# An attention and mixture-of-experts kernel: experts in the order of their token counts, with 448, 416 or 384 slots by place, and addresses from a register

## The chip, the cores and the metric

The kernel runs on one core of one Trainium2 chip. The metric is device time in microseconds of one execution. A run of three executions and one profiled execution are shown; an execution's time is some microseconds more than its span in the profile, which goes from the first to the last instruction.

The engines are named as in the profile: PE (TensorE, matmuls; PEld is its weight load), DVE (VectorE), ACT (ScalarE), POOL (GpSimd) and SP (SyncE, which here only issues DMAs and reads registers). L75 is line 75 of the kernel before.

## The reference

A gated linear attention gives x, and a mixture of eight experts with one expert per token follows. Cut to what matters:

```python
# attention: q, k, v, a_re, a_im are (4, 8, 768, 48)
for t in range(S):                       # state S_re, S_im: (B, H, D, D)
    S_re, S_im = ar * S_re - ai * S_im + outer(k[t], v[t]), ar * S_im + ai * S_re
    y[:, :, t] = einsum('bhd,bhde->bhe', q[:, :, t], S_re)
x = y.transpose(0, 2, 1, 3).reshape(3072, 384)
# experts: w_gate (384, 8), w1 (8, 384, 1024), w2 (8, 1024, 384)
logits = x @ w_gate
expert_idx = argmax(logits, axis=1)
gate_w = softmax(logits)[arange(N), expert_idx]
for e in range(8):
    rows = expert_idx == e
    out[rows] = gate_w[rows] * (relu(x[rows] @ w1[e]) @ w2[e])
```

`setup_inputs()` sets the seed 0, so the inputs are always the same. All data are float32.

## The kernel before

**Attention.** The 3072 tokens are 24 tiles of 128, taken in pairs ("units", 12 of them). Each unit's decays and angles are summed with matmuls against triangular matrices, q and k are scaled and rotated, and chunk scores, outputs and the running state are made by matmuls. A tile's output is transposed into rows of x (tile `x`) and multiplied by the gate weights (`logits`, L341), whose four matmuls write four strips of 32 partitions.

**Routing.** Four tiles form a group, six groups in all. `choose` (L352) finds each token's expert (`fst`) and its gate weight (`gt`); `route` (L373) counts tokens per expert with one-hot rows, running sums in `cx` and two matmuls into `rps`, and gives each token a row of the DRAM table `xs`: expert times 448 plus its rank. `put` (L407) scatters the rows of a tile to `xs` with an indirect DMA on POOL, four puts a group. The last group is routed when the experts have begun: the first 256 rows of the first expert (`FIRST`) are gathered before it, and `base` makes sure that late tokens get ranks from 256 on.

**Experts.** Every expert has `CAP` = 448 slots, as three tiles of 128 and one of 64, and the experts run in the order 0 to 7. For each of them `gather` (L488) reads its rows from `xs` into `xg`, `turn` (L589) transposes them on PE (tile `tp`) and copies them to `xt`, and `expert` (L615) runs two layers. The first makes eight tiles `hps` of 128 hidden units by 448 tokens, three matmuls each, with relu into `ht` on ACT and DVE in turn. The second makes one tile `yps` per 128 tokens, eight matmuls of 384 columns each. In the tile of 64 tokens the eight matmuls are split over two halves of the output partitions, four in each, which a copy on ACT and an add on DVE bring together (L646, L647). DVE multiplies by the gate weight, and `scatter` (L605) writes the rows to the output with an indirect DMA on POOL. The first expert is run in two parts, of 256 and 192 slots.

**Weights.** An expert's weights are 1.5 MB for `w1t` and 1.5 MB for `w2t`, in two sets of buffers. Those of expert 0 come in seven DMAs, one per unit from the fifth to the eleventh unit (L566); those of expert 1 before the experts start; the others two experts ahead, each buffer as soon as its last reader has ended (L712). All of these, the inputs and the gathers go through SP's queue, in one order that a scheduler sets from the order of the program.

**Checks on the side.** `range_check` (L666) tests the inputs' range on ACT and POOL while experts 1 to 6 run. `verdict` (L685) joins its result and the tokens that found no slot (`ov`) into `flag`, with one small matmul (`bp`). After the last expert every engine reads `flag`; if it isn't zero, spare code runs (`slow_attention`, `others`), which takes each expert over all 24 tiles. 

## Time and profile before

| | |
|---|---|
| Runs before | 620.66 us median of 3 (620.58 to 621.86) |
| Profiled execution | 620.54 us, span 618.8 us, 8535 instructions, granted PE clock 0.988 |
| PE busy | 563.5 us (91%), 3319 records; PEld 369.7 (60%) |
| DVE, ACT, POOL busy | 264.6 (43%), 284.5 (46%), 104.0 (17%) |
| DMA | 79.73 MB, mean 129 GB/s |
| `hps` matmuls | 148.4 us busy, 432 records |
| `yps` matmuls | 147.2 us busy, 512 records |

A float32 matmul leaves two records in the trace, so 432 records of `hps` are 216 matmuls. The busy time of a group counts overlapping records once, while the mean of one record has the time in which it overlaps with the next; so the cost of a matmul is read from the starts of consecutive blocks, not from that mean. A timeline row gives start, length, engine, line, operation, tile, shapes and the number of records merged; what stands in brackets is idle time ahead and what ended it. In a row of stretches the numbers in parentheses count instructions, and behind POOL stand the granted PE clock (1.00 is 2.4 GHz, 0.50 is 1.2 GHz), the mean busy share of the 16 DMA engines and GB/s.

### The profile page before, as it was taken

To read this page: it belongs to the slowest core of one execution; us is meant where nothing else is said; L and a number is where in the kernel's file an instruction comes from. 1 tells how busy PE (TensorE), PEld (TensorE's weight loads), DVE (VectorE), ACT (ScalarE), POOL (GpSimd) and SP (SyncE) were. 2 spreads that over 40 slices of the span, in tenths; PEclk is the share of its full clock that TensorE was granted. 3 is DMA by queue.
4 is the path that set the end of the run, shared out by engine and by line. 5 is a ranking of instruction groups with operands and counts; after the bars stand their busy time and mean duration, and the time that the engine had idled before them with its cause. 6 is when DMAs were issued, how large, how long until landed. Compare 5 with 4: busy or idle time off the path is not lost. (4 is left out here: it accounts for less than half of the span.)

```text
span 618.8 us, 8535 instructions
## 1 busy us (share of the span) xinstructions
PE 563.5 (91%) x3319; PEld 369.7 (60%) x3319; DVE 264.6 (43%) x579; ACT 284.5 (46%) x479; POOL 104.0 (17%) x100
## 2 busy tenths in 40 slices
PE   1498799899899899998899999999999999999993
PEld 0176588677677677776766554555555555455551
DVE  2567787787787779781312112121121211211111
ACT  6558876865865866743101161341613416134100
POOL 1000000100200200302120042140521405214011
PEclk9999999999999999999799999999999999999997
DMA  9996965575476251161125636426364263610000
GB/s 183 208 263 129 269 144 99 137 149 109 111 142 118 77 117 27 43 215 53 51 73 176 229 114 236 140 62 228 114 236 138 64 225 114 239 40 33 2 13 32
DMA packets 154232, 79.73 MB, mean 129 GB/s; under 512 B 130230, under 2 KB 145735, under 8 KB 154184
## 3 DMA queue, kind: packets, MB, share of 16 engines
q1 hardware_dynamic: 147008, 69.48, 43.7%
q0 software_dynamic: 3456, 9.47, 4.4%
q10 hardware_dynamic: 3720, 0.16, 0.3%
q8 instruction: 28, 0.46, 0.3%
q14 instruction: 20, 0.16, 0.1%
HBM read 63.74 MB, written 15.98 MB: 129 GB/s over the span
## 5 line engine op out<-in xcount | busy, mean ns | idle before, releaser
L75 PE MATMUL hps<-xt,w1t 128*128 128x448 f32 (+2 forms) x432 | 148.4, 504 | 0.0
L75 PE MATMUL yps<-w2t,ht 128*128 128x384 f32 (+1 forms) x512 | 147.2, 488 | 0.3 <-DVE y L639 0.3
L75 PEld LDWEIGHTS yps<-w2t,ht 128*128 128x128 f32 (+1 forms) x512 | 81.4, 177 | 64.4 <-issue 15.0
L75 PEld LDWEIGHTS hps<-xt,w1t 128*128 128x128 f32 x432 | 80.7, 192 | 61.9 <-issue 59.0
L624 ACT ACTIVATE ht<-hps 128x448 f32<-128x448 f32 (+2 forms) x36 | 18.1, 502 | 137.0 <-PE hps L75 137.0
L408 POOL DMA_INDIRECT xs<-x,to x24 | 26.6, 1107 | 284.4 <-DMA fl<-f 109.4
L639 DVE TENSOR_SCALAR y<-yps,xg 128x384 f32<-128x384 f32 x24 | 14.8, 617 | 118.4 <-PE yps L75 118.4
L628 DVE TENSOR_SCALAR ht<-hps 128x448 f32<-128x448 f32 (+2 forms) x36 | 20.6, 573 | 104.3 <-PE hps L75 103.0
L75 PE MATMUL at<-qt,kt 96*128 96x128 f32 x384 | 53.5, 282 | 0.8 <-ACT kt L78 0.7
L75 PEld LDWEIGHTS at<-qt,kt 96*128 96x128 f32 x384 | 47.9, 192 | 10.2 <-DVE kt L78 3.1
L75 PE MATMUL y<-am,v 128*64 128x128 f32 x384 | 50.6, 285 | 3.5 <-DVE am L438 3.4
L606 POOL DMA_INDIRECT out_dram<-y,xg x32 | 30.9, 966 | 94.1 <-DVE y L639 45.3
L438 DVE TENSOR_TENSOR am<-at,tri 128x512 f32<-128x512 f32 x48 | 33.0, 688 | 26.2 <-PE at L75 26.2
L75 PE MATMUL y<-qt,G 96*64 96x128 f32 x320 | 42.9, 278 | 0.0
L75 PE MATMUL csl<-A,tri_half 128*128 128x384 f32 x48 | 24.2, 590 | 20.5 <-DVE A L248 17.9
L677 POOL TENSOR_TENSOR cs<-cs,cw 128x768 f32<-128x768 f32 x12 | 21.6, 1804 | 117.4 <-ACT cw L673 117.4
L430 PE MATMUL tp<-ident,Q 128*96 128x128 f32 x192 | 33.7, 285 | 8.1 <-DVE Q L338 6.8
L75 PEld LDWEIGHTS y<-am,v 128*64 128x64 f32 x384 | 31.6, 135 | 14.4 <-issue 7.7
L78 ACT COPY qt<-tp 96x512 f32<-96x512 f32 x48 | 27.5, 583 | 21.5 <-PE tp L430 21.3
L201 ACT ACT_TABLE_LOAD x27 | 34.6, 1283 | 2.0 <-PEq L858 0.8
L430 PE MATMUL tp<-ident,K 128*96 128x128 f32 x192 | 30.8, 279 | 1.5 <-DVE K L338 1.5
L75 PE MATMUL dk<-v,K 128*96 128x48 f32 x320 | 32.2, 253 | 0.0
(122 smaller groups left out, 715.3 us busy)
## 6 DMA issues: line engine op xcount, KB each, us to landing
w1t<-in_moe_w_dram SPq DMA_DIRECT2D x7, 1536.0 KB
w2t<-in_moe_w_dram SPq DMA_DIRECT2D x7, 1536.0 KB
xs<-zrow SPq DMA_DIRECT2D x7, 772.0 KB
ar<-in_a_re_dram SPq DMA_DIRECT2D x12, 384.0 KB
ai<-in_a_im_dram SPq DMA_DIRECT2D x12, 384.0 KB
q<-in_q_dram SPq DMA_DIRECT2D x12, 384.0 KB
k<-in_k_dram SPq DMA_DIRECT2D x12, 384.0 KB
v<-in_v_dram SPq DMA_DIRECT2D x12, 384.0 KB
```

The costliest lines, as they stand in the source:

```text
L75: return nc.tensor.matmul(o, lhsT=lhsT, rhs=rhs, start=start, stop=stop, skip_group_check=True)
L78: (nc.scalar.copy if i % 2 else nc.vector.tensor_copy)(out=o, in_=in_)
L201: ins = nc.scalar.preload_act_table_set(name)
L408: pool(nc.gpsimd.indirect_dma_start(out=xs[:, :], out_offset=bass.IndirectOffsetOnAxis(ap=to[:, i : i + 1], axis=0), in_=x[:, i], in_offse ...
L430: nc.tensor.transpose(out=tp[0:DD, j], in_=X[:, hg * 4 + j], identity=ident)
L438: nc.vector.tensor_tensor(out=am, in0=at, in1=bc(tri, 1, 4), op=OP.mult)
L606: return nc.gpsimd.indirect_dma_start(out=out, out_offset=bass.IndirectOffsetOnAxis(ap=idx, axis=0), in_=y[0:m], in_offset=None, bounds_ch ...
L624: relu = nc.scalar.activation(out=ht[:, f], in_=ps, func=AF.Relu)
L628: nc.vector.tensor_scalar(out=ht[:, f], in0=ps, scalar1=0.0, scalar2=None, op0=OP.max)
L639: nc.vector.tensor_scalar(out=y, in0=ps, scalar1=gate, scalar2=None, op0=OP.mult)
L677: nc.gpsimd.tensor_tensor(out=s, in0=s, in1=w, op=OP.add)
```

## The change

The experts no longer run in the order of their numbers. A ranking by token counts sets the order, and the place in it sets the slots: `CAPS` = 448 for the first two, 416 for the next three, 384 for the last three. The table `xs` keeps 448 rows per expert.

- `rank` makes the order on DVE, on one partition, in some ten small steps: it compares all counts with each other, sums to a place per expert, and turns places into a list of experts. It runs twice. The first time, in the routing of the fourth group, it takes the counts of the first 16 tiles and fixes the first two experts (`order` 0); `bonus` keeps them ahead in the second ranking, which takes all counts (`used`) after the last group and fixes the other six (`order` 1). One small matmul into a further column of `rps` gives the counts each time.
- `experts_at` reads the numbers of the experts into registers of SP, two before the first weights, six after the first expert has been written into the program. `load_w` and `gather` address weights and rows by these registers.
- The first expert's weights are no longer spread over seven units: they are all loaded in the last unit, behind the two register loads.
- A place with 416 slots has a last tile of 32 tokens. `expert` splits its eight matmuls over four strips of 32 partitions, two in each, and joins them by a copy and three adds. A place with 384 slots has three full tiles and no other.
- `verdict` also flags an expert that has more tokens than its place has slots. `route` keeps the token's row in `slot` for the spare code, which is adapted and not shown here.

```diff
+    CAPS = [CAP] * 2 + [CAP - 32] * 3 + [CAP - 64] * 3
+    BIG = 32768.0
...
+    ex = []
+
+    def rank(cnt, some):
+
+        tt = nc.vector.tensor_tensor
+        key = xl.tile([1, E], FP, tag="key", name="key")
+        nc.vector.scalar_tensor_tensor(out=key, in0=cnt, scalar=8.0, in1=rev[0:1], op0=OP.mult, op1=OP.add)
+        if not some:
+            tt(out=key, in0=key, in1=bonus, op=OP.add)
+        w = xl.tile([1, E, E], FP, tag="kw", name="kw")
+        tt(out=w, in0=bc(key, 1, E), in1=bc(key, 2, E), op=OP.is_gt)
+        nc.vector.reduce_sum(place_of, w, axis=AX_X)
+        if some:
+            nc.vector.tensor_scalar(
+                out=bonus, in0=place_of, scalar1=-BIG, scalar2=2.0 * BIG, op0=OP.mult, op1=OP.add
+            )
+            nc.vector.tensor_scalar(out=bonus, in0=bonus, scalar1=0.0, scalar2=None, op0=OP.max)
+        w = xl.tile([1, E, E], FP, tag="kw", name="kw")
+        tt(out=w, in0=bc(place_of, 1, E), in1=bc(eid[0:1], 2, E), op=OP.is_equal)
+        tt(out=w, in0=w, in1=bc(eid[0:1], 1, E), op=OP.mult)
+        key = xl.tile([1, E], FP, tag="key", name="key")
+        nc.vector.reduce_sum(key, w, axis=AX_X)
+        nc.vector.tensor_copy(out=order[not some], in_=key)
+
+    def experts_at(i, some):
+
+        for e in i:
+            ex.append(nc.values_load(order[not some][0:1, e : e + 1], engines=[mybir.EngineType.SP], min_val=0, max_val=E - 1))
+
     def load_w(e, parts=None):
...
-        w1e, w2e = w1[e].rearrange("(i p) f -> p i f", p=P), w2[e].rearrange("(i p) d -> p i d", p=P)
+        w1e, w2e = [w[ds(ex[e], 1)].rearrange("o (i p) f -> p (o i) f", p=P) for w in (w1, w2)]
...
             mm(ps[:, n], ones_b, cx[:, j])
...
+            mm(ps[0:1, n + 1], ones_b[:, 0:1], cx[:, NT])
...
-        to = xl.tile([P, n], I32, tag="to", name="to")
+        to = slot[:, sl]
         stt(out=to, in0=far, scalar=float(NS), in1=rk, op0=OP.add, op1=OP.add)
+        if j == NT - 3 * GR:
+            mm(ps[0:1, n + 1], ones_b[:, 0:1], cx[:, j + n])
+            rank(ps[0:1, n + 1], True)
...
+        def last():
+            tt(out=used, in0=ps[0:1, n + 1], in1=base[0:1], op=OP.subtract)
+            rank(used, False)
...
-        return [lambda i=i: put(i) for i in range(n)]
+        return [lambda i=i: put(i) for i in range(n)] + ([last] if end else [])
...
-    def gather(s, sizes):
+    def gather(e, s, sizes):
...
-        nc.sync.dma_start(out=xg[:, :f], in_=xs[s : s + f * P].rearrange("(i p) c -> p i c", p=P))
+        rows = xs[0:NS].rearrange("(e s) c -> e s c", s=CAP)[ds(ex[e], 1), s : s + sum(sizes)]
+        nc.sync.dma_start(out=xg[:, :f], in_=rows[:, : f * P].rearrange("o (i p) c -> p (o i) c", p=P))
         if f < n:
-            nc.sync.dma_start(out=xg[0 : sizes[f], f], in_=xs[s + f * P : s + f * P + sizes[f]])
+            nc.sync.dma_start(out=xg[0 : sizes[f], f], in_=rows[:, f * P :].rearrange("o p c -> (o p) c"))
...
-        if NU - 8 <= u < NU - 1:
-            load_w(0, [u - (NU - 8)])
+        if u == NU - 1:
+            experts_at(range(2), True)
+            load_w(0, range(KD + KF // 2))
...
-                for f in range(KF // 2):
-                    for z in range(2):
-                        g = z * (KF // 2) + f
-                        mm(ps[z * HT : (z + 1) * HT], h[:, g], wb[:, g], f == 0, f == KF // 2 - 1)
-                nc.scalar.copy(out=y[0:m], in_=ps[HT : HT + m])
-                nc.vector.tensor_tensor(out=y[0:m], in0=ps[0:m], in1=y[0:m], op=OP.add)
+                zs = P // m
+                for f in range(KF // zs):
+                    for z in range(zs):
+                        g = z * (KF // zs) + f
+                        mm(ps[z * m : (z + 1) * m], h[:, g], wb[:, g], f == 0, f == KF // zs - 1)
+                nc.scalar.copy(out=y[0:m], in_=ps[m : 2 * m])
+                for z in [0] + list(range(2, zs)):
+                    nc.vector.tensor_tensor(out=y[0:m], in0=ps[z * m : (z + 1) * m], in1=y[0:m], op=OP.add)
...
+        for i in (2, 5):
+            w = xl.tile([1, E], FP, tag="key", name="key")
+            ts(out=w, in0=place_of, scalar1=float(i), scalar2=32.0, op0=OP.is_ge, op1=OP.mult)
+            nc.vector.tensor_tensor(out=used, in0=used, in1=w, op=OP.add)
+        ts(out=used, in0=used, scalar1=float(CAP), scalar2=None, op0=OP.is_gt)
...
+        nc.vector.reduce_sum(over, used, axis=AX_X)
+        nc.vector.tensor_tensor(out=two[0:1, 1:2], in0=two[0:1, 1:2], in1=over, op=OP.add)
...
-            part = [(own, xg)]
+            part = [(tiles(CAPS[e]), xg)]
...
-                xg = gather((e + 1) * CAP, own)
+                xg = gather(e + 1, 0, tiles(CAPS[e + 1]))
...
             expert(sizes, xt, *W_T[e], g, todo)
+        if e == 0:
+            experts_at(range(2, E), False)
         if e + 2 < E:
             load_w(e + 2)
```

**How it moves instructions on SP.** These are SP's rows where the attention ends, from the last load of v on. `w1t` and `w2t` with all parts in one DMA (128x3x1024, 128x8x384) are the second expert's weights, `xg` with 128x2x386 is the first gather, `own0`, and the two `xg` rows behind it are the gather of the first expert's second part. Before:

```order
L215 DMA v_96<-in_v_dram 128x16x48
L166 DMA w1t<-in_moe_w_dram 128x3x1024
L167 DMA w2t<-in_moe_w_dram 128x8x384
L493 DMA xg<-xs 128x2x386
L493 DMA xg<-xs 128x386
L495 DMA xg<-xs 64x386
```

Now (of the seven DMAs of the first expert's weights the first, and of the six register loads the first):

```order
L253 DMA v_96<-in_v_dram 128x16x48
L193 TENSOR_LOAD order_122
L193 ISA x2
...
L209 ISA
L209 DMA w1t<-in_moe_w_dram 128x1024
...
L540 DMA xg<-xs 128x2x386
L204 ISA
L204 DMA w1t<-in_moe_w_dram 128x3x1024
L205 ISA
L205 DMA w2t<-in_moe_w_dram 128x8x384
L193 TENSOR_LOAD order_123
...
L540 DMA xg<-xs 128x386
```

The first expert's weights have come down from the attention to this place, behind the register loads; the second expert's weights, which stood ahead of `own0`, stand behind it; and six register loads stand ahead of the gather of the second part.

**On DVE, the fourth group's routing.** `rk`, `ov`, `far` and `to` (now `slot`) are `route`'s own steps; `key`, `kw`, `place`, `bonus` and `order` belong to `rank`; `am`, `Qe`, `Ke`, `A` and `r` are the attention's. Before:

```order
L395 TENSOR_REDUCE rk<-ro 128x4
L396 TENSOR_SCALAR ov<-rk 128x4
...
L403 SCALAR_TENSOR_TENSOR to<-far,rk 128x4
L333 TENSOR_TENSOR Qe<-q,E 128x384
L333 TENSOR_TENSOR Ke<-k,Ei 128x384
L243 SCALAR_TENSOR_TENSOR A<-A,R 128x768
L308 TENSOR_SCALAR r<-cst 128x384
```

Now:

```order
L434 TENSOR_REDUCE rk<-ro 128x4
L172 SCALAR_TENSOR_TENSOR key<-rps,rev 1x8
...
L184 TENSOR_TENSOR kw<-place,eid 1x64
L442 SCALAR_TENSOR_TENSOR slot<-far,rk 128x4
L182 TENSOR_SCALAR bonus<-bonus 1x8
L185 TENSOR_TENSOR kw<-kw,eid 1x64
L371 TENSOR_TENSOR Qe<-q,E 128x384
L187 TENSOR_REDUCE key<-kw 1x8
L371 TENSOR_TENSOR Ke<-k,Ei 128x384
L281 SCALAR_TENSOR_TENSOR A<-A,R 128x768
L346 TENSOR_SCALAR r<-cst 128x384
L188 CAST order_122<-key 1x8
```

The ranking's steps are woven into `route`'s and the attention's, and its last one, the CAST that SP waits for, stands behind the step `r<-cst`.

**On PE, between the fourth and the seventh place.** `bp` is the verdict's matmul. Before, from the transposes of one expert to the verdict:

```order
L595 MATMUL tp<-ident,xg 128x128 x3
L595 MATMUL tp<-ident,xg 128x64
L75 MATMUL hps<-xt,w1t 128x448 x24
L75 MATMUL yps<-w2t,ht 128x384 x24
L75 MATMUL yps<-w2t,ht 64x384 x8
L75 MATMUL bp<-two,ones 1x2
```

Now, the last two places with 416 and 384 slots ahead of the verdict:

```order
L79 MATMUL hps<-xt,w1t 128x416 x24
L79 MATMUL yps<-w2t,ht 128x384 x24
L79 MATMUL yps<-w2t,ht 32x384 x8
L643 MATMUL tp<-ident,xg 128x128 x9
L79 MATMUL hps<-xt,w1t 128x384 x24
...
L79 MATMUL yps<-w2t,ht 128x384 x24
L79 MATMUL bp<-two,ones 1x2
```

The tiles of 64 tokens have become tiles of 32 in three places and are gone in three, and the verdict's matmul stands right behind full tiles.

## Rows read from the trace of the kernel before

**Rows 1.** Stretches by stage: us, busy (instructions) per engine, PEclk, DMA, GB/s.
```profile
50.00:297.52 247.52, 228.33 (x2163) 180.79 (x2160) 185.10 (x415) 166.93 (x289) 22.69 (x20) 0.99 0.53 120
...
339.73:608.90 269.17, 268.09 (x859) 142.66 (x858) 43.95 (x79) 81.31 (x136) 70.47 (x52) 1.00 0.37 130
...
608.90:618.80 9.90, 0.00 (x0) 0.00 (x0) 0.96 (x2) 0.47 (x1) 0.91 (x1) 0.61 0.05 16
```

**Rows 2.** PE in time order, one 448-slot expert: start, us, line, op, tile.
```profile
339.73 18.31 PE L75 MATMUL hps<-xt,w1t 128*128 128x448 f32 x48
357.88 18.37 PE L75 MATMUL yps<-w2t,ht 128*128 128x384 f32 x64
376.18 2.22 PE L595 MATMUL tp<-ident,xg 128*128 128x128 f32 x12
378.33 18.31 PE L75 MATMUL hps<-xt,w1t 128*128 128x448 f32 x48
```

**Rows 3.** PE in time order, the first expert's two parts.
```profile
309.55 10.48 PE L75 MATMUL yps<-w2t,ht 128*128 128x384 f32 x32
...
319.87 0.94 PE L595 MATMUL tp<-ident,xg 128*128 128x128 f32 x4
...
321.68 8.07 PE L75 MATMUL hps<-xt,w1t 128*128 128x192 f32 x48
...
329.59 8.05 PE L75 MATMUL yps<-w2t,ht 128*128 128x384 f32 x32
```

**Rows 4.** PE in time order, attention: the logits' four-strip matmuls and the next.
```profile
260.84 0.42 PE L75 MATMUL lt<-xt,wg 128*32 128x128 f32 x8
261.20 0.44 PE L75 MATMUL y<-am,v 128*64 128x128 f32 x4
261.46 0.39 PE L75 MATMUL y<-qt,G 96*64 96x128 f32 x4
```

**Rows 5.** SP's DMA issues in time order, around the first expert.
```profile
238.71 0.37 SPq L215 DMA_DIRECT2D v<-in_v_dram  x1
...
292.82 23.84 SPq L493 DMA_DIRECT2D xg<-xs  x2
...
316.70 0.51 SPq L495 DMA_DIRECT2D xg<-xs  x1
```

**Rows 6.** DVE in time order: route's last step, fourth group and last group.
```profile
240.63 0.15 DVE L403 SCALAR_TENSOR_TENSOR to<-far,rk 128x4 int32<-128x4 f32 x1
...
242.67 0.55 DVE L308 TENSOR_SCALAR r<-cst 128x384 f32<-128x384 f32 x1
...
302.54 0.16 DVE L403 SCALAR_TENSOR_TENSOR to<-far,rk 128x4 int32<-128x4 f32 x1
```

**Rows 7.** Line 838's instructions on SP: ns min/median/max, first and last start.
```profile
L838 SPq TENSOR_LOAD <-flag x1: 473/473/473, 569.9 to 569.9; - x1
...
L838 SPq FUSED_REGOPS  x1: 191/191/191, 570.5 to 570.5; - x1
```

**Rows 8.** The stretch in which the second expert's weights arrive.
```profile
265.50:276.50 11.00, 10.31 (x103) 8.28 (x102) 10.05 (x31) 6.84 (x12) 0.00 (x0) 1.00 0.82 286
```

**Rows 9.** POOL in time order: first and last of the last group's four puts.
```profile
303.46 0.97 POOL L408 DMA_INDIRECT xs<-x,to  x1 [14.41 <-DVE to L403]
...
313.64 0.97 POOL L408 DMA_INDIRECT xs<-x,to  x1 [2.39 <-DMA xs<-x,to]
```

**Rows 10.** All engines in time order: the verdict, and the end.
```profile
565.81 0.18 DVE L687 TENSOR_SCALAR bad<-bad 128x24 f32<-128x24 f32 x1 [8.96 <-ACT cai L673]
...
606.20 0.62 DVE L639 TENSOR_SCALAR y<-yps,xg 128x384 f32<-128x384 f32 x1 [4.54 <-PE yps L75]
...
610.03 0.41 DVE L648 TENSOR_SCALAR y<-y,xg 64x384 f32<-64x384 f32 x1
```

**Rows 11.** Stretches of 4 us where the attention ends.
```profile
290.00:294.00 4.00, 2.12 (x26) 1.35 (x22) 0.35 (x2) 1.29 (x3) 0.00 (x0) 0.95 0.11 21
294.00:298.00 4.00, 2.08 (x8) 1.59 (x9) 1.18 (x6) 0.50 (x2) 0.00 (x0) 0.50 0.28 95
```

More of the change, by code (lines that the diff above doesn't have):

```diff
@@ L127 @@
     nc.gpsimd.iota(rev, pattern=[[-1, E]], base=E, channel_multiplier=0, allow_small_or_imprecise_dtypes=True)
+    eid = const([P, E], "eid")
+    nc.gpsimd.iota(eid, pattern=[[1, E]], base=0, channel_multiplier=0, allow_small_or_imprecise_dtypes=True)
+    place_of, used, bonus = [const([1, E], nm) for nm in ("place", "used", "bonus")]
+    order = [const([1, E], f"order{i}", I32) for i in range(2)]
+    slot = const([P, NT], "slot", I32)
     tid = const([P, NT], "tid")
@@ L381, in route @@
             tt(out=cx[:, j + i + 1], in0=cx[:, j + i], in1=oh[:, i], op=OP.add)
-        ps = psL.tile([P, n + 1, E], FP, tag="mm", padded_shape=[P, 64, E], name="rps")
+        ps = psL.tile([P, n + 2, E], FP, tag="mm", padded_shape=[P, 64, E], name="rps")
         rp = ps[:, :n].rearrange("p j e -> p (j e)")
@@ L570 @@
         f()
-    own0 = gather(0, [P] * (FIRST // P))
+    own0 = gather(0, 0, [P] * (FIRST // P))
     choose(NT - GR, GR)()
@@ L696, with tiles @@
     flag = const([1, 2], "flag", I32)
-    rest0 = [P] * ((CAP - FIRST) // P) + [HT]
-    own = [P] * (CT - 1) + [HT]
+    def tiles(n):
+        return [P] * (n // P) + [n % P] * (n % P > 0)
     for e in range(E):
         if e == 0:
-            part = [([P] * (FIRST // P), own0), (rest0, gather(FIRST, rest0))]
+            rest0 = tiles(CAPS[0] - FIRST)
+            part = [([P] * (FIRST // P), own0), (rest0, gather(0, FIRST, rest0))]
         else:
-            part = [(own, xg)]
+            part = [(tiles(CAPS[e]), xg)]
         for i, (sizes, g) in enumerate(part):
@@ L810, in others @@
             nc.vector.memset(ec, float(E))
-            me, far = [mo.tile([P, NT], FP, name=nm) for nm in ("me", "far2")]
+            me, far, row = [mo.tile([P, NT], FP, name=nm) for nm in ("me", "far2", "row")]
             fr, to = [mo.tile([P, NT], I32, name=nm) for nm in ("fr", "to2")]
@@ L814, in others @@
             nc.vector.tensor_scalar(out=far, in0=tid, scalar1=-float(N), scalar2=None, op0=OP.add)
+            nc.vector.tensor_copy(out=row, in_=slot)
+            nc.vector.tensor_scalar(out=row, in0=row, scalar1=-float(ZR), scalar2=None, op0=OP.add)
             with tc.For_i(0, E, 1) as ev:
@@ L819, in others @@
                 nc.sync.dma_start(out=wb, in_=w2[ds(ev, 1)].rearrange("o (i p) d -> p (o i) d", p=P))
[L820 to L823 removed]
+                for o, w, z in ((fr, row, ZR), (to, far, N)):
+                    nc.vector.scalar_tensor_tensor(out=me, in0=fst, scalar=ec, in1=w, op0=OP.is_equal, op1=OP.mult)
+                    nc.vector.tensor_scalar(out=o, in0=me, scalar1=float(z), scalar2=None, op0=OP.add)
                 nc.vector.tensor_scalar(out=ec, in0=ec, scalar1=-1.0, scalar2=None, op0=OP.add)
@@ L836, in others @@
                     expert([P], turn([P], xg), wa, wb, xg)
-    with tc.If(nc.values_load(flag[0:1, 1:2], min_val=0, max_val=P * (2 * NC + NT)) > 0):
+    with tc.If(nc.values_load(flag[0:1, 1:2], min_val=0, max_val=P * (2 * NC + NT) + E) > 0):
         with tc.If(nc.values_load(flag[0:1, 0:1], min_val=0, max_val=P * 2 * NC) > 0):
             slow_attention()
-            nc.vector.memset(ov, 1.0)
+            nc.vector.tensor_scalar(out=slot, in0=tid, scalar1=float(NS), scalar2=None, op0=OP.add)
             choose(0, NT)()
```

6 lines of the change are left out of this document (2 added, 4 removed).

## The prediction

> **What bounds the kernel now.** I read the stretches by stage first [rows 1]: in 339.73 to 608.90 us TensorE is busy 268.09 of 269.17 us at full granted clock while DVE is busy 43.95 and DMA engines have a share of 0.37. So in the experts each column that TensorE is spared is time off the end. In the attention (50 to 297.52) it is busy 228.33 of 247.52, with DVE and ACT close behind: a shared bound. Next TensorE in time order over one 448-slot expert [rows 2]: `hps` starts at 339.73, `yps` at 357.88, the transposes at 376.18, the next `hps` at 378.33. The period is 38.60 us: 18.15 for the 24 `hps` matmuls (a row counts two records for each), 18.30 for `yps`, 2.15 for the transposes. No gap stands in it.
>
> **Will the smaller places hold the tokens?** The inputs are fixed by a seed, so I counted with the reference: 421, 406, 403, 392, 388, 370, 354, 338 tokens, in falling order. Places of 448, 448, 416, 416, 416, 384, 384, 384 hold them. The first two are picked from the first 16 of 24 tiles, where the leaders have 279, 274 and then 272: these are the experts with 406 and 421, so no place overflows.
>
> **Term 1, `hps`: -11.5.** 448 columns take 18.15 / 24 = 756 ns [rows 2]; 192 columns, in the first expert's second part, take (329.59 - 321.68) / 24 = 330 ns [rows 3]. That is 1.667 ns a column. 32 columns less save 24 x 53.3 ns = 1.28 us, in three experts; 64 less save 2.56, in three: 3.84 + 7.68.
>
> **Term 2, half tiles that vanish: -8.5.** 16 full `yps` matmuls run from 309.55 to 319.87 [rows 3], 0.645 us each, so three full tiles take 15.48 and the half tile the other 18.30 - 15.48 = 2.82. Three experts with 384 slots have none.
>
> **Term 3, half tiles that become quarter tiles: -3.9.** The same eight matmuls now fill four strips of 32 output partitions, not two of 64. No row shows four strips with 384 columns. The bounds: no gain (2.82 stays), if only two run abreast; half of 2.82 saved, 1.41, if four do. The nearest row is the logits' matmul, four strips of 32 with 128 columns [rows 4]: the four take 0.36 us (260.84 to 261.20), where two 64-wide ones take 0.26 (261.20 to 261.46). Two by two they would need 0.52, so four do go abreast, with 0.1 for the four weight loads. I take 1.3, three times. The Trainium skill, TensorEngine Tiling (Array Packing), section Performance Considerations, speaks against this step: tiling speeds TensorE but not the evacuation of PSUM, which may become the bottleneck after a fourfold split. That rule is priced as a rival below.
>
> **Term 4, transposes: -0.9.** Nine full ones instead of nine and three halves, and copies of 384 columns: 2.15 x 64 / 448 = 0.3 each for three experts. Bounds 0 and twice that.
>
> **Weights of the first expert: 0.** Today seven DMAs are spread over the attention; now they leave together on SP after two register loads, which wait for DVE's ranking of the first 16 tiles. SP's last load before that goes out at 238.71 [rows 5], so SP is free. The ranking's last step stands behind the `r<-cst` step, which ends at 243.2 [rows 6]; eleven small steps of 0.15 to 0.19 us put it at 245 at the latest. A register load takes 0.47, with its arithmetic 0.8 (569.9 to 570.7) [rows 7]: 247. The second expert's weights, equally 3.1 MB, came in within 11 us at 286 GB/s under attention work [rows 8]; with seven issues the first expert's are there near 262. They are needed at 297.5. 35 us of cover. Taking 3.1 MB out of the earlier attention may save SP and DMA time; I bound that by 0 and -2 and take 0, since TensorE's partners there are DVE and ACT.
>
> **Second expert's weights and the queue they join: 0.** They stood ahead of the first gather (`own0`) and now stand behind it, so they start near 293.5 [rows 5] and end by about 304.5. They are needed near 340. Behind them SP does six register loads, 6 x 0.8 = 4.8 us, after the final ranking (an estimate: 304.5, ten small steps behind 302.7): done before 310. Next on SP is the gather of the first expert's second part, which waits for the last group's four puts anyway.
>
> **Term 5, that gather: +0.6.** `route`'s last step ends at 302.70 [rows 6], the puts start at 303.46 and the last at 313.64 [rows 9], the second DMA of the gather goes out at 316.70 [rows 5], and TensorE wants the rows at 319.87 [rows 3], with no idle time ahead. The cover is small. The final ranking puts five steps between `route`'s own on DVE: 0.4 us, as they fill half of its gaps. The second DMA gets a register step of 0.19. If there is no slack left, that is 0.6. Bounds: 0, and a whole put period more ((313.64 - 303.46) / 3 = 3.4) if the end of the weights' transfer holds up the first put.
>
> **Term 6, ranking in the attention: +0.5.** Eleven steps of at most 0.19 on DVE: 0 to 2.1. DVE is busy 185 of 247 us there [rows 1], so most fall into gaps.
>
> **Term 7, the verdict: +0.3.** Its matmul stands right behind the sixth place's full tiles instead of behind a half tile, and its operand gets one more add. DVE's chain starts at 565.81, on ACT's range check [rows 10]; TensorE would reach the matmul near 566.5 and find the operand near 567.0, after six small steps and a multiply. Bounds 0 and 0.6; I take the middle.
>
> **Term 8, the end: -0.8.** TensorE stops at 608.9 [rows 1]; copy, add and multiply of the half tile end at 610.44; a full tile needs one multiply of 0.62 [rows 10].
>
> **The sum.** -11.5 - 8.5 - 3.9 - 0.9 + 0.6 + 0.5 + 0.3 - 0.8 = -24.2. The profiled execution took 620.54 us (its span 618.8 and 1.7 around it); the runs' median is 620.66, 0.1 above. Forecast: 620.5 - 24.2 = **596.3 us**. A measurement of this kernel can tell about 0.2%, 1.2 us, from no change.
>
> **Rivals.**
> - *Strips by pairs.* Term 3 gives nothing: 600.2. Against it stands the step of 0.36 [rows 4]; for it, that 384 columns were never seen in four strips. 7%.
> - *Evacuation takes over.* A quarter tile needs a copy and four DVE steps of up to 0.62 [rows 10], 2.5 us beside 1.5 of matmuls. If the next expert had to wait for the difference, 3 x 1.0: 599.3. Against it: DVE is busy 16% of this stage [rows 1], the next `yps` bank is wanted 18 us later, and `hps` has three banks. 3%. This is the skill's rule named at term 3; DVE's 16% does not bear it out.
> - *The second part stalls and the clock falls.* In 290 to 294 TensorE was busy 2.12 of 4 us, and in 294 to 298 the granted clock was 0.50, the level of 1.2 GHz [rows 11]: 2 us of work lost in these four, some 3 in all. With the upper bound of term 5 (3.4 more) there would be such a hole at 320: 596.3 + 3.4 + 3 = 602.7. Against it: the matmuls around are dense. 5%.
> - *Less DMA helps the attention.* -2: 594.3 or a little less. 2%.
> - *Slower: first weights late.* If the seven DMAs crawl, `hps` at 297.5 waits for all of them. To lose 24 + 1.2 us they would have to land after 322.7, under 42 GB/s from 247 on. At 21 GB/s, what the engines moved in 290 to 294 [rows 11], 3.1 MB take 150 us: landing at 397, 99 us late, 695. Against it: 286 GB/s [rows 8]; 21 is what was asked for there, not what could be had. 2%.
> - *The change does not do what it says.* If rounding turned two of the near tokens, another expert could come second and one with 421 tokens sit in a place of 416; the verdict then starts the spare path, which takes all 8 experts over 24 single tiles: 192 x (24 x 128 x 1.667 ns + 8 x 0.645 us) = 192 x 10.3, about 2000 us more. Leads of 2 and 13 tokens speak against it. 2%.
>
> **How the numbers follow.** 79% remain for the forecast, with its terms inside their bounds. All terms at their best (term 3 at -4.2, term 4 at -1.8, no losses) give 593.6, but not all together; I set the lower end at 594.4. The upper end, 600.8, takes in the pairs (600.2) and the evacuation (599.3), and about half of the bounds of terms 5 and 6. Left out: the clock, the two slow cases, and little tails, under 20%. Slower: 2 + 2 = 4%; within 0.2%: 1%; faster: 95%.
>
> **What would show it.** Right: `hps` groups of 416 and 384 columns with periods near 36.0 and 32.9 us; quarter tiles of about 1.5 us; no TensorE wait on the first expert's weights; the ranking's CAST near 244. Wrong: `tp` of the first expert's second part waiting more than 1 us for `xg` (term 5), quarter tiles near 2.8 (term 3), a new clock dip near 320, or the verdict's matmul holding the transposes for more than a microsecond.

## The result, and the profile after

The changed kernel takes **595.22 us** (median of 4 runs, 594.55 to 596.49), the kernel before, run beside it, 621.26 (620.58 to 622.07): a ratio of 0.9583, 95% interval 0.956 to 0.9605. Forecast were 596.3 us, 594.4 to 600.8. The profiled execution took 594.93 us, its span 593.2, so 25.6 less than the span before. In the second of the three series taken of the change one execution ran slow (714.77 us at a granted clock of 0.763); its time is left out everywhere, but it is the execution that this series has a profile of.

The page of the kernel after: its span, the first line of busy times, and the two groups of matmuls.

```profile
span 593.2 us, 8521 instructions
...
PE 536.9 (91%) x3264; PEld 362.8 (61%) x3264; DVE 265.9 (45%) x604; ACT 282.1 (48%) x476; POOL 100.1 (17%) x98
...
L79 PE MATMUL hps<-xt,w1t 128*128 128x416 f32 (+4 forms) x432 | 136.6, 476 | 0.0
L79 PE MATMUL yps<-w2t,ht 128*128 128x384 f32 (+2 forms) x464 | 135.1, 487 | 0.0
```

The stretches of the kernel after that answer to [rows 1], in the same columns: attention up to the first expert's transposes, second expert to PE's last matmul, the tail.

```profile
50.00:297.86 247.86, 228.44 (x2166) 180.78 (x2166) 184.36 (x420) 168.27 (x290) 21.39 (x20) 1.00 0.56 111
341.66:584.65 242.99, 241.34 (x802) 136.34 (x801) 43.55 (x81) 79.18 (x134) 67.69 (x49) 1.00 0.41 142
584.65:593.20 8.55, 0.00 (x1) 0.00 (x0) 0.62 (x1) 0.00 (x0) 0.97 (x1) 0.72 0.05 18
```

The balance is read off the edges. Seven experts took 269.17 us and take 242.99: -26.18. The tail went from 9.90 to 8.55: -1.35. Everything ahead of the second expert got longer: its first `hps` stood at 339.73 and stands at 341.66, +1.93. Together -25.6. PE is nearly as full in the experts as before (241.34 of 242.99, where it was 268.09 of 269.17), so the gain is columns and not waits.

PE of the kernel after in time order, at the places of [rows 2, 3]; in brackets idle time ahead and what ended it. The row at 520.20 is cut short by the end of the view's stretch.

```profile
297.86 0.73 PE L643 MATMUL tp<-ident,xg 128*128 128x128 f32 x4 [2.04 <-DMA xg<-xs]
...
321.79 0.97 PE L643 MATMUL tp<-ident,xg 128*128 128x128 f32 x4
...
380.17 17.03 PE L79 MATMUL hps<-xt,w1t 128*128 128x416 f32 x48
397.03 17.07 PE L79 MATMUL yps<-w2t,ht 128*128 128x384 f32 x64
414.03 2.13 PE L643 MATMUL tp<-ident,xg 128*128 128x128 f32 x12
...
487.46 15.65 PE L79 MATMUL hps<-xt,w1t 128*128 128x384 f32 x48
502.95 15.64 PE L79 MATMUL yps<-w2t,ht 128*128 128x384 f32 x48
518.43 0.82 PE L643 MATMUL tp<-ident,xg 128*128 128x128 f32 x6
519.81 0.55 PE L643 MATMUL tp<-ident,xg 128*128 128x128 f32 x3 [0.57 <-ACT xt L82]
520.20 2.10 PE L79 MATMUL hps<-xt,w1t 128*128 128x384 f32 x6
...
535.68 15.64 PE L79 MATMUL yps<-w2t,ht 128*128 128x384 f32 x48
551.83 0.19 PE L79 MATMUL bp<-two,ones 128*1 128x2 f32 x2 [0.50 <-DVE two L751]
551.95 1.02 PE L643 MATMUL tp<-ident,xg 128*128 128x128 f32 x6
...
553.53 15.65 PE L79 MATMUL hps<-xt,w1t 128*128 128x384 f32 x48
```

A place of 416 slots takes 397.03 - 380.17 = 16.86 us for `hps`, 17.00 for `yps`, and its successor's transposes follow. A place of 384 takes 15.49 and 15.48. The quarter tile is what 17.00 has above 15.48: 1.52, where the half tile took 2.82.

DVE of the kernel after: the cast that SP waits for, a step of the last angles that carries the turn over from the chunk before, and the last multiply.

```profile
245.12 0.15 DVE L188 CAST order<-key 1x8 int32<-1x8 f32 x1
...
258.28 0.16 DVE L302 SCALAR_TENSOR_TENSOR c<-fl,c 96x8 f32<-96x8 f32 x1 [1.75 <-DMA c<-ai]
...
584.69 0.62 DVE L687 TENSOR_SCALAR y<-yps,xg 128x384 f32<-128x384 f32 x1 [4.54 <-PE yps L79]
```

SP's issues after, which answer to [rows 5]: the first expert's seven DMAs, the first gather, the gather of its second part.

```profile
246.89 1.46 SPq L209 DMA_DIRECT2D w1t<-in_moe_w_dram  x3
248.54 2.21 SPq L209 DMA_DIRECT2D w2t<-in_moe_w_dram  x4
294.33 0.37 SPq L540 DMA_DIRECT2D xg<-xs  x1
...
318.96 0.59 SPq L542 DMA_DIRECT2D xg<-xs  x1
```

POOL after: two puts of the fourth group, and the first of the last group's ([rows 9]).

```profile
249.41 1.12 POOL L454 DMA_INDIRECT xs<-x,slot  x1 [31.42 <-DVE kt L82]
257.60 0.97 POOL L454 DMA_INDIRECT xs<-x,slot  x1 [7.08 <-DMA xs<-x,slot]
...
305.32 0.97 POOL L454 DMA_INDIRECT xs<-x,slot  x1 [13.47 <-DVE kw L185]
```

The ranking and the register loads come when forecast: the cast at 245.12 (245), the first weights' DMA at 246.89 (247). Two things were not forecast. DVE waits 1.75 us for ScalarE's little transfer `c<-ai` (3 KB, from the angles' row to 96 partitions), which is under way while the weights pour in; in the kernel before, DVE had its step at 254.93 without a wait. And the second put stands idle 7.08 us, where that gap was 3.55. A third shows when the two traces are laid side by side from their start: the first unit's step `Qe` on DVE begins at 15.87 us before and 17.21 after, far ahead of anything the diff computes.

One thing must be known to compare single executions. Where the attention ends, the clock drops to 0.50 ([rows 11]); by the trace this lasted 6.8 us in the profile before and 3.4 in this one, and it changes from execution to execution of one kernel (6.8 in the change's third profile). Each run's mean granted clock tells the two apart, but not fully: in three of the profiles below (the order alone, two strips, all three edits) a further drop of 3.4 us stands near 53 us. Among kernels that end alike I therefore also compare runs of like clock, as a rougher measure than the ratios.

### The profile page after: what moved, and what is told of

Its sections match the earlier page's. It is cut to its first block, busy times and chain, and to the rows that moved or that the text cites. A ratio compares the mean times of both kernels' runs of the same rounds, so it can differ in the third digit from the quotient of the medians.

```text
span 593.2 us, 8521 instructions
## 1 busy us (share of the span) xinstructions
PE 536.9 (91%) x3264; PEld 362.8 (61%) x3264; DVE 265.9 (45%) x604; ACT 282.1 (48%) x476; POOL 100.1 (17%) x98
## 4 chain that ended last, share of the span: by engine, by line
PE 77%; DVE 10%; DMA 5%; ACT 3%; issue 2%; POOL 1%; SPq 0%; POOLq 0%; DVEq 0%; ACTq 0%
PE hps L79 23%; PE yps L79 20%; PE at L79 6%; PE y L79 6%; PE tp L476 6%; PE dk L79 5%; PE cst L79 3%; PE csl L79 3%; PE tp L643 2%; DMA xs<-x,slot 2%; DVE r L346 2%; PE tpx L526 1%; DVE f L347 1%; DVE am L484 1%; PE lt L79 1%
## 5 line engine op out<-in xcount | busy, mean ns | idle before, releaser
L79 PE MATMUL hps<-xt,w1t 128*128 128x416 f32 (+4 forms) x432 | 136.6, 476 | 0.0
L79 PE MATMUL yps<-w2t,ht 128*128 128x384 f32 (+2 forms) x464 | 135.1, 487 | 0.0
L79 PEld LDWEIGHTS yps<-w2t,ht 128*128 128x128 f32 (+2 forms) x464 | 76.3, 178 | 56.7 <-issue 7.4
L672 ACT ACTIVATE ht<-hps 128x416 f32<-128x416 f32 (+4 forms) x36 | 17.1, 476 | 125.9 <-PE hps L79 121.5
L454 POOL DMA_INDIRECT xs<-x,slot x24 | 25.3, 1054 | 287.6 <-DMA ai<-in_a_im_dram 110.7
L676 DVE TENSOR_SCALAR ht<-hps 128x416 f32<-128x416 f32 (+4 forms) x36 | 19.4, 539 | 89.2 <-PE hps L79 87.9
L79 PE MATMUL csl<-A,tri_half 128*128 128x384 f32 x48 | 24.2, 590 | 21.8 <-DVE A L286 18.7
L654 POOL DMA_INDIRECT out_dram<-y,xg x29 | 28.1, 970 | 91.7 <-DVE y L687 42.1
L476 PEld LDWEIGHTS tp<-ident,Q 128*96 128x96 f32 x192 | 20.8, 131 | 18.6 <-issue 9.1
```

Of the source, the lines that this page charges most:

```text
L79: return nc.tensor.matmul(o, lhsT=lhsT, rhs=rhs, start=start, stop=stop, skip_group_check=True)
L454: pool(nc.gpsimd.indirect_dma_start(out=xs[:, :], out_offset=bass.IndirectOffsetOnAxis(ap=to[:, i : i + 1], axis=0), in_=x[:, i], in_offse ...
L476: nc.tensor.transpose(out=tp[0:DD, j], in_=X[:, hg * 4 + j], identity=ident)
L654: return nc.gpsimd.indirect_dma_start(out=out, out_offset=bass.IndirectOffsetOnAxis(ap=idx, axis=0), in_=y[0:m], in_offset=None, bounds_ch ...
L672: relu = nc.scalar.activation(out=ht[:, f], in_=ps, func=AF.Relu)
L676: nc.vector.tensor_scalar(out=ht[:, f], in0=ps, scalar1=0.0, scalar2=None, op0=OP.max)
```

## The experiments

Each is the change with one edit, unless said otherwise. The times, with means over the runs of like granted clock:

| kernel | median (runs) | ratio to before, 95% | clock 0.993-0.994 | clock 0.990-0.991 |
|---|---|---|---|---|
| the change, three series | 595.22, 596.98, 597.32 | 0.9583, 0.9609, 0.9611 | 594.84 (6) | 596.69 (4) |
| input tiles moved by 32 bytes | 595.07 (5) | 0.9574 [0.9553, 0.9594] | 593.83 (2) | 595.13 (2) |
| those and v's tiles | 593.84 (5) | 0.9572 [0.9548, 0.9596] | 593.51 (3) | 595.47 (1) |
| weights behind the carry step | 596.21 (5) | 0.9588 [0.9574, 0.9603] | 595.71 (3) | 596.51 (2) |
| v's tiles + verdict later | 594.90 (5) | 0.9589 [0.9566, 0.9611] | 593.62 (2) | 595.34 (2) |
| v's tiles + weights later | 593.88 (5) | 0.9560 [0.9538, 0.9581] | 592.82 (2) | 594.48 (3) |
| all three | 594.18 (5) | 0.9554 [0.9533, 0.9575] | none | 593.57 (5) |

The first four experiments ran on one chip, the three with 32 bytes and the one with the weights behind the carry step on a second, the last four on a third (that of the change's first series is not on record). The kernel before took 620.57 us on the first and 621.68 on the second at the same clock of 0.991 (3 and 6 runs), so about a microsecond between times from different chips is not told apart by the two columns on the right; the ratios are each to the kernel before on the same chip.

**The change again.** No edit; is the late start chance?

> The changed kernel once more, unaltered, to see what one and the same program varies by. The shift of 1.3 us that DVE shows against the kernel before in the first 16 us, where both programs do the same work, is chance by my theory: then this run's step Qe of the first unit stands anywhere between 15.9 and 17.2 us, and the median is 595.2 within 1. Rival: the change itself delays the start (more constants, other code); then that step stands at 17.2 again within 0.1.

596.98 us (four runs), ratio 0.9609 [0.9579, 0.9639]; `Qe` starts at 17.24. Chance fell, and what the change does to the start became the question.

**The order alone.** All places with 448 slots:

```diff
-    CAPS = [CAP] * 2 + [CAP - 32] * 3 + [CAP - 64] * 3
+    CAPS = [CAP] * E
```

> The change with 448 slots in all eight places: order, register addresses and late first weights alone. My theory: the places give all of the gain (some 26 us) and the order costs between 0.5 and 2: 621 to 623, ratio to the kernel before 1.000 to 1.004, with the period of an expert 38.6 us as before. Rival: the order and the late weights bring something by themselves, as they take 3.1 MB of weights out of the middle of the attention: below 619.5. Second rival: they cost more than 3 us, and the smaller places give more than 26: above 624.

623.43 us, ratio 1.0032 [1.0015, 1.0049], 0.4 us above the range I gave. Ranking, registers, weights in one burst and whatever delays the start cost 2 us together; the smaller places alone bring the ratio from 1.0032 to 0.958 to 0.961. `Qe` starts at 17.39 here too.

**Two strips instead of four** in the tile of 32 tokens:

```diff
-                zs = P // m
+                zs = 2
```

> The last tile of 32 tokens in the 416-slot places is split over two strips of 32 output partitions, not four: eight matmuls, four in each strip, and one add. My theory, four strips do run abreast: each such tile takes 2.8 us where the change takes 1.5, so 3 x 1.3 = 3.9 us more, 599.1. Rival, the strips go two by two in both: no change in time, 595.2, tile at 1.5 as now.

600.79 us, ratio 0.9669 [0.9646, 0.9691], where 599.1 had been reckoned from the first series alone; 600.63 (3 runs) at a clock of 0.990 to 0.991, 3.9 above the change. PE of this kernel in time order, the `yps` of a place with 416 slots and the next transposes:

```profile
400.34 18.35 PE L79 MATMUL yps<-w2t,ht 128*128 128x384 f32 x64
418.62 2.13 PE L643 MATMUL tp<-ident,xg 128*128 128x128 f32 x12
```

18.28 us instead of 17.00: 1.28 a place, 3.84 in three. Term 3 is the four strips, and they run four abreast with 384 columns as with 128.

**No place of 384 slots**:

```diff
-    CAPS = [CAP] * 2 + [CAP - 32] * 3 + [CAP - 64] * 3
+    CAPS = [CAP] * 2 + [CAP - 32] * 6
```

> Places of 448, 448 and six times 416. My theory: time goes by the columns and tiles of TensorE alone, so the last three places get the period of a 416-slot place (35.92 us, where 384 slots take 32.6): some 3 x 3.2 = 9.7 us more, 604.9. Rival: the smaller places are bounded by something else too (the range check on ACT and POOL, the verdict, weights): then less than 6 us are lost, under 601.

609.15 us, ratio 0.9809 [0.9787, 0.9832], 4 us over my figure. A place of 416 runs 35.92 us from `hps` to `hps` and one of 384 takes 32.74, 9.5 in three, as expected; PE ends 10.6 later than in the change (595.24 for 584.65), of which 0.4 is from ahead of the second expert and 0.7 from the verdict and the transposes. What I had not counted is behind PE's end, in the last tile. DVE of this kernel there:

```profile
593.85 0.62 DVE L687 TENSOR_SCALAR y<-yps,xg 128x384 f32<-128x384 f32 x1 [4.54 <-PE yps L79]
595.80 1.73 DVE L697 TENSOR_TENSOR y<-yps,y 32x384 f32<-32x384 f32 x3 [1.34 <-ACT y L695]
597.57 0.41 DVE L698 TENSOR_SCALAR y<-y,xg 32x384 f32<-32x384 f32 x1
```

The copy, three adds and the multiply put the last scatter at 598.72, 3.5 us behind PE's end, where the change has it 0.9 behind. The tail is 11.36 us instead of 8.55. So joining strips is free between experts, where `yps` of the next is far off, and is paid in full at the end: the Trainium skill says in TensorEngine Tiling (Array Packing), section Performance Considerations, that tiling does not speed the evacuation of PSUM. The trace agrees (the three adds take 1.73 us here), and in this kernel that costs something only behind the last matmul.

**The place of the input tiles.** The late start needed a cause that the order alone has too. The change adds small tiles ahead of those that take the inputs, 288 bytes of constants and 576 of the routing's, per partition. In the built programs the first tile of `ar` begins at byte 109184 before and at 110048 after: a multiple of 64, and 32 past one. The inputs come as 192-byte packets. Three kernels, all with one unused tile of 32 bytes: the change with it ahead of the input tiles, the kernel before with it in the same place, and the change with it ahead of v's tiles, which begin at 32 past a multiple of 64 in the kernel before as well.

```diff
+    pad = ld.tile([P, 8], FP, tag="pad", name="pad", bufs=1)
+    nc.vector.memset(pad, 0.0)
```

> The changed kernel with one unused tile of 32 bytes per partition ahead of the tiles that the input goes to. The change's new small tiles add up to 864 bytes ahead of them, so that these tiles begin at 32 bytes past a multiple of 64 and not at a multiple of 64, as before; with the 32 bytes they begin at one again. Theory (the place of the input tiles in SBUF makes the 192-byte input packets slower): the packets of the first stretch take a mean of 19 to 21 ns and not 23 to 24, the first unit's step on VectorE that now starts at 17.2 us starts at 15.8 to 16.0, and the kernel takes 1.3 us less than the change: about 594 us median, 0.957 of before. Rival (the longer program or its first instructions delay the start): that step stays at 17.2 us and the time at 595.5 to 597.

> The kernel before with the same 32 bytes alone, and nothing of the change: its input tiles now begin at 32 bytes past a multiple of 64. Theory (place in SBUF): the step on VectorE moves from 15.9 to 17.2 us and the kernel takes 1.3 us more, a ratio of 1.002 to 1.003. Rival (the program's length): step at 15.9 us and ratio 1.000.

> The changed kernel with the 32 bytes further ahead, before the three tiles of v, which begin at 32 bytes past a multiple of 64 in the kernel before too: now the tiles of v and those of the other four inputs all begin at a multiple of 64. Theory: a fifth of the input packets, those of v, get faster too, so the input is through earlier than in the kernel before; the step on VectorE starts at 15.9 us or earlier. If the attention waits for input later than that step, another 0 to 1 us goes: 593 to 594.3 us. Rival: as the run with the tile behind v, or no change at all (595.5 to 597).

The view of DMA in the stretch 10 to 30 us, queue q1 (SP's: packets, MB, share of 16 engines), for five kernels. Before:

```profile
q1 hardware_dynamic: 21701, 4.07, 137.6%
```

The kernel before with the 32 bytes:

```profile
q1 hardware_dynamic: 19133, 3.58, 143.9%
```

The change:

```profile
q1 hardware_dynamic: 19134, 3.58, 142.5%
```

The change with the 32 bytes ahead of the input tiles:

```profile
q1 hardware_dynamic: 21695, 4.07, 134.6%
```

The change with them ahead of v's:

```profile
q1 hardware_dynamic: 23218, 4.36, 122.8%
```

Share x 16 engines x 20 us / packets is the mean time of a packet: 20.3, 24.1, 23.8, 19.9 and 16.9 ns. (The share passes 100% since packets of one engine overlap.) It follows the place and not the program: 32 bytes turn the change into the kernel before, and the kernel before into the change. The start goes along. DVE's first `Qe` in the kernel before and in the same with the 32 bytes:

```profile
15.87 0.56 DVE L333 TENSOR_TENSOR Qe<-q,E 128x384 f32<-128x384 f32 x1 [3.87 <-ACT E L189]
```

```profile
17.30 0.56 DVE L336 TENSOR_TENSOR Qe<-q,E 128x384 f32<-128x384 f32 x1 [4.61 <-ACT E L189]
```

and in the change with the 32 bytes, where it had been at 17.21:

```profile
15.90 0.56 DVE L374 TENSOR_TENSOR Qe<-q,E 128x384 f32<-128x384 f32 x1 [3.73 <-ACT E L227]
```

In time, the clean pair is the kernel before with and without the 32 bytes, on one chip: 622.56 us beside 621.91, 0.65 more, ratio 1.0016 [1.0004, 1.0029], a little less than the 1.002 to 1.003 expected. In the change it is worth 1.0 us (594.84 to 593.83) and 1.6 (596.69 to 595.13) at like clocks, but with two runs each and from different chips; the medians alone (595.07 beside 595.22, 596.98 and 597.32) do not show it. So it costs time, and these pairs put it at 0.6 to 1.6 us. With v's tiles in place too it is 1.3 at a clock of 0.993, with the same reserve. The expected median of 594 us was met by the last only: the shorter clock drop came in two and three of five runs.

**First weights behind the carry step.** The cast that ends the first ranking is queued on DVE behind the last step that carries an angle, so that the burst begins after `c<-ai`:

```diff
-        nc.vector.tensor_copy(out=order[not some], in_=key)
+        def out():
+            ins = nc.vector.tensor_copy(out=order[not some], in_=key)
+            if some:
+                queue(ins, T["carry"])
...
                 if i == 1:
                     carry_angle(u)
+                    if "first" in T:
+                        T.pop("first")()
```

> The changed kernel with one line more: the cast that ends the first ranking stands on VectorE behind the last step that carries an angle, so that the seven transfers of the first expert's weights leave SP behind ScalarE's small transfer and not under it. Theory (the burst holds that small transfer for some 2.7 us, VectorE waits 1.7 us, GpSimd's second put later): ScalarE's transfer is back to some 1.5 us, VectorE's wait at 258 us goes, and the kernel takes 0.6 us less than the change. Rival (the wait has slack): no change in the time, or the weights come too late for the first matmuls that read them at 300 us and it costs up to 1 us.

No gain shows: 595.71 against 594.84 at a clock of 0.993, 596.51 against 596.69 at 0.991. The wait it was aimed at is gone (DVE of this kernel):

```profile
257.50 0.15 DVE L311 SCALAR_TENSOR_TENSOR c<-fl,c 96x8 f32<-96x8 f32 x1
```

but SP's issues now begin at 259.35,

```profile
259.35 1.46 SPq L218 DMA_DIRECT2D w1t<-in_moe_w_dram  x3
```

and ScalarE's second transfer, back from the 96 partitions, is issued at 259.9 by the rows of the tile `c`. By the trace's packets it runs from 263.71 to 265.05, under the weights; in the change, issued at 258.9, it ran from 260.05 to 260.25, just behind them. PE's `cst`, which needs it, comes at 265.72 for 264.44, 1.28 later than in the change, of which 0.43 stood there at 259 us. The wait was not removed but moved to the second of two transfers. The edit also turned a few neighbouring steps of PE and DVE around.

**Weights behind both transfers, verdict behind the transposes, and both**, on top of the 32 bytes ahead of v:

```diff
+            if some:
+                queue(ins, T["r"])
...
+                if c == 0 and "first" in T:
+                    T.pop("first")()
```

```diff
             xt = turn(sizes, g)
+            if e == E - 1:
+                verdict()
...
-        if e == E - 2:
-            verdict()
```

> The run with the 32 bytes before v, and the cast that ends the first ranking queued on VectorE behind the first range step r of the last angles, so that the first expert's seven weight transfers leave SP behind both of ScalarE's small transfers (the angles to the 96 partitions, and back). Theory (the run with the cast behind the carry step alone only moved the collision from the first to the second of these): both take under 1.6 us, no wait of TensorE or VectorE at 255 to 267 us is longer than in the kernel before, and the kernel takes 0.6 to 0.8 us less, about 592.8 us at a clock of 0.993. Rival (the weights collide with the puts or with the second expert's): the gain is given back before 300 us, no change.

> The run with the 32 bytes before v, and the verdict called behind the last expert's transposes, so that the matmul bp that waits for VectorE's verdict stands behind the 9 transposes on TensorE and not ahead of them. Theory (TensorE waits 0.50 us for the verdict at 551.8 us with nothing else to do): that wait goes, 0.5 us less, about 593.0 us against 593.5 for the other at the same granted clock of 0.993. Rival (the wait only moves to the first matmuls of the last expert): no change.

> Aligned input tiles, verdict behind the transposes, first weights behind both small transfers: all that the study found, in one kernel. If they add: 593.5 - 0.5 - 0.7 = 592.3 us at a clock of 0.993, and 2.7 us less than the change (595.1 at that clock); a ratio to before of 0.952 to 0.956.

Weights behind both: 592.82 at 0.993, 0.7 less than without (593.51, on another chip), as expected; beside the run with the verdict later, on the same chip, it is 0.8 less at 0.993 (593.62) and 0.9 at 0.990 to 0.991 (594.48 for 595.34), with two or three runs each. The ratios of all runs overlap (0.956 [0.9538, 0.9581] and 0.9589 [0.9566, 0.9611]). DVE's carry step has no wait, at 255.93 and not 257.35 as in the same kernel without, and the issues begin where no small transfer runs (SP of this kernel):

```profile
266.41 1.45 SPq L220 DMA_DIRECT2D w1t<-in_moe_w_dram  x3
```

Verdict later: the times don't tell it (593.62 against 593.51). The trace does. PE of this kernel in time order, the last row cut short by the end of the view's stretch:

```profile
534.10 15.64 PE L79 MATMUL yps<-w2t,ht 128*128 128x384 f32 x48
549.58 0.82 PE L645 MATMUL tp<-ident,xg 128*128 128x128 f32 x6
550.97 0.55 PE L645 MATMUL tp<-ident,xg 128*128 128x128 f32 x3 [0.57 <-ACT xt L82]
551.45 0.19 PE L79 MATMUL bp<-two,ones 128*1 128x2 f32 x2
551.57 2.85 PE L79 MATMUL hps<-xt,w1t 128*128 128x384 f32 x8
```

From `yps` to the next `hps` it is 17.47 us, where the change has 17.85 (535.68 to 553.53) and a place without the verdict 17.25 (502.95 to 520.20). The wait of 0.50 for the verdict is gone: from `yps` to the matmul behind it are 15.48 us instead of 16.15. The transposes take 0.29 more (1.87 for 1.58), with a longer wait for their own copy (0.57 for 0.17), and 0.4 is left as gain.

Both together with the 32 bytes: 594.18 us, ratio 0.9554 [0.9533, 0.9575], beside the change on the same chip at 597.32, 0.9611 [0.9581, 0.964]. The intervals don't touch. At a clock of 0.990 to 0.991 it is 3.1 us less than the change, and 2.8 less than the change's one run of that clock on the same chip (596.32), where 2.7 were expected; its profile has two drops of 3.4 us and not one of 6.8, so this is not quite like beside like. The 592.3 at 0.993 stays untested, as no run had that clock. This is the fastest kernel of the study.

**The change a third time**:

> The changed kernel itself once more, beside the three above on one chip: 595 to 597 us, ratio 0.956 to 0.961; the step on VectorE of the first unit at 17.2 us as in both earlier profiles, if the place of the input tiles sets it. At 38 to 43 us the profiles of the change and of its variants differ by up to 1 us at equal addresses: this one shows whether that is the execution's or the kernel's.

597.32 us, ratio 0.9611, both just above the range. DVE's first `Qe` starts within 0.1 us of the first profile. At 39 us the two profiles of one kernel stand 0.41 apart, so differences of that size there are the execution's. This profile has the long clock drop, and the second expert's first layer starts 1.37 us later than in the first profile:

```profile
343.03 18.31 PE L79 MATMUL hps<-xt,w1t 128*128 128x448 f32 x48
```

## Why the prediction was right

The forecast was 596.3 us, the change took 595.22, 596.98 and 597.32 in three series. The terms in us, against the first profile after:

| term | forecast | measured | from |
|---|---|---|---|
| 1, `hps` | -11.5 | -11.9 | 3 x (18.15 - 16.86) + 3 x (18.15 - 15.49) |
| 2, half tiles gone | -8.5 | -8.4 | 18.30 - 15.48 = 2.82, twice; 2.73 at the end |
| 3, quarter tiles | -3.9 | -3.9 | 3 x (2.82 - 1.52) |
| 4, transposes | -0.9 | -1.8 | 2.15 to 2.06 (416 slots), to 1.58 or 1.77 (384) |
| 7, verdict | +0.3 | -0.3 | below |
| 8, the end | -0.8 | -1.35 | tail 9.90 to 8.55 |
| 5, 6, first weights | +1.1 | +1.9 | second expert's `hps` 339.73 to 341.66 |
| sum | -24.2 | -25.6 (unrounded) | spans: -25.6 |

**Terms 1 to 3** carry the forecast and hold within 0.4 us. Term 1 was scaled from 192 columns; from 448 to 384 columns the slope is 2.66 / 24 / 64 = 1.73 ns a column, not 1.667. Term 3 rested on a row with 128 columns [rows 4], and the run with two strips shows that it carries over. The rival "strips by pairs" (600.2) is what that run is: 600.6. "Evacuation takes over" did not come: behind a quarter tile PE goes on to the next transposes without a wait. The gaps that it has there, 0.3 to 0.6 us, are waits for the copies of the transposes themselves, and they are the same with two strips.

**Term 4** was undersized because I scaled it by columns. A transpose costs by the piece: twelve pieces took 2.15 with a half tile and 2.06 with a quarter tile, the nine of a place of 384 take 1.58 to 1.77. **Term 8** was undersized as well. The prediction's own rows give 1.54 - 0.62 = 0.92 and not 0.8, and it took only ACT's and DVE's steps into account; the last scatter starts 0.94 us behind PE's end, not 1.97, and what follows it took 0.3 less. POOL's last scatter before and after:

```profile
610.87 0.91 POOL L606 DMA_INDIRECT out_dram<-y,xg  x1 [2.81 <-DVE y L648]
585.59 0.97 POOL L654 DMA_INDIRECT out_dram<-y,xg  x1 [4.19 <-DVE y L687]
```

**Term 7** had the wrong sign. The wait itself came as forecast: `yps` to `bp` was 18.64 against 18.30 without a verdict, and is 16.15 against 15.48, 0.33 more. But the transposes behind it had taken 2.74 us before instead of 2.15, and now take what they take elsewhere (1.58): 0.59 less, which I had not looked at. PE of the kernel before there:

```profile
550.87 15.64 PE L75 MATMUL yps<-w2t,ht 128*128 128x384 f32 x48
...
569.51 0.19 PE L75 MATMUL bp<-two,ones 128*1 128x2 f32 x2
569.63 1.44 PE L595 MATMUL tp<-ident,xg 128*128 128x128 f32 x8
...
572.37 18.31 PE L75 MATMUL hps<-xt,w1t 128*128 128x448 f32 x48
```

**Terms 5 and 6 and the first weights** came to +1.9 and not +1.1, and that is flattered by the clock. With the 6.8 us drop of the profile before, the change's third profile has the second expert's `hps` at 343.03: +3.3. Its span, 594.55, lies 24.2 below the span before, the forecast to the tenth, and that is luck: terms 4, 7 and 8 took 2 us more off than forecast, and what lies ahead of the second expert cost 2.2 more. By the profiles with the same drop:

| kernel | second expert's `hps` | above before |
|---|---|---|
| before | 339.73 | |
| before, input tiles moved by 32 bytes | 342.00 | 2.3 |
| the change | 343.03 | 3.3 |
| the change, weights behind the carry step | 343.29 | 3.6 |
| the change, input tiles back | 341.82 | 2.1 |
| the same with v's, weights behind both transfers | 341.10 | 1.4 |

Term 5 was 0: the second part's transposes start 10.37 us behind the `yps` block ahead of them, without a wait (321.79), as in [rows 3] (10.32). The step that failed is the one that priced the first expert's weights at **0, "35 us of cover"**. The cover is there for TensorE, which never waits for the weights. It was not asked who else moves data in those 11 us: a 3 KB transfer that DVE waits for. That burst costs some 0.7 to 0.9 us by the run that moves it away (at like clocks, few runs each; 2.1 to 1.4 in the table has v's tiles in it as well), while the run that moves it half way moves the wait along: the wait and its cause are shown, the size roughly. And a cost that no term held, 0.6 to 1.6 us, comes from the addresses of tiles that the diff doesn't name. The 1.4 that is left can't be laid to anything for sure. The table has one execution a kernel, and the kernel before with the 32 bytes stands 2.3 above in it where its runs are 0.65 slower: two profiles alone can be a microsecond or more apart. At 39 us, ahead of any ranking, 0.66 of the 1.4 is there already (DVE's `am` at 39.13 for 38.47), and 0.8 comes only in the first expert, where the clock drop now falls (at the first transposes it is +0.60, 296.38 for 295.77). What the ranking itself costs (term 6, +0.5) is not shown: of the 1.9 us that the order alone costs, the addresses and the burst leave between nothing and half a microsecond.

So the forecast was right by the terms that carried it; three errors of half a microsecond to a microsecond (terms 4, 7, 8) and two unseen losses of about one each went against each other, and that they nearly cancelled is luck.

## What to carry to other kernels

When work is sorted by size, price the smaller sizes from blocks of the same trace and keep an unpadded size for the last place, since the joining of strips is hidden everywhere but there. When a large transfer is moved to a stretch with "enough cover", list the small transfers of other queues in that stretch and who waits for them, all of them, not only the first. When tiles are added ahead of others, look where the tiles with small packets begin: here 32 bytes of padding were worth about a microsecond, 0.6 to 1.6 in the pairs above.

## What the runs showed of the hardware

**Where a tile begins in SBUF sets the time of its small packets.** The packets of SP's queue, 97% of them of 192 bytes, into tiles that begin at a multiple of 64 bytes took a mean of 16.9 ns in 10 to 30 us, into tiles 32 bytes past one 23.8 and 24.1, and with v alone out of place 19.9 and 20.3. The other profiles agree: 15.9 to 16.9 in all four kernels with every tile in place, 23.8 to 24.1 in all eight with none in place. The Trainium skill, DMA: Bandwidth & Descriptors, section How a descriptor splits into AXI transactions, says that a descriptor which doesn't begin at a multiple of 256 bytes also pays for the bytes below its start. It says so of what is read, and here the side that moved is the one written, so its use here is a guess. An estimate from that page, with pieces 192 bytes apart in four inputs and 256 bytes apart in v: a mean of 8.4 beats of 32 bytes a packet with all in place, 9.8 with v out of place, 10.6 with all out. The order agrees with the trace (16.9; 19.9 and 20.3; 23.8 and 24.1 ns); the steps are larger in it, 18 to 20% and 41% for 17% and 26%. Whether the multiple of 64 or the distance to 256 decides, these places don't tell apart.

**A burst delays a small transfer of another queue.** ScalarE's 3 KB transfer has 112 packets. By the trace they passed within 0.34 us in the kernel before and in 1.25 under the weights' burst, and the last one landed at 257.82, 5.1 us after its issue at 252.7. Moved behind the burst's start, the second such transfer took 5.1 us as well (259.91 to 265.05), where it had taken 1.4. In seven more profiles with the burst in that place the first transfer took 5.1 to 5.3 us, and 1.5 in all five in which the burst doesn't meet it.
